# V of B by one load per head, with an 8 KB source element over four 2 KB destination rows

One core of one Trainium2 chip. The metric is the device time of one execution in microseconds (us), best read as the median of several; "the kernel before" and "the change" are run in turn on the same chip. The sets of experiments ran on different chips, so across sets only the ratios to "before" are compared. A run more than 1.5% above the fastest of its kernel is called slow and is left out of the ratios.

## The reference, cut to what matters

Two attention blocks read a key/value cache; their outputs are concatenated. Block A has 4 K/V heads shared by 32 query heads; block B has 32 heads, each with its own K and V, and it is B that moves the bytes.

```python
# B: x (16, 32, 1024), k_cache and v_cache (16, 32, 1024, 128), all bf16
q = (x @ wq).reshape(B, Sq, H, Dh).transpose(0, 2, 1, 3)
scores = jnp.einsum("bhqd,bhkd->bhqk", q, k_cache) * (Dh ** -0.5)
p = softmax(scores)
o = jnp.einsum("bhqk,bhkd->bhqd", p, v_cache)
return o.transpose(0, 2, 1, 3).reshape(B, Sq, H * Dh) @ wo
# ... A the same, with k and v repeated over 8 query heads; result = concatenate([A, B], -1)
```

K of B and V of B are 134 MB each; all else that is read comes to 69 MB.

## The kernel before: the parts that matter

The kernel does 128 steps. Each step handles one batch entry and four heads of B (and a piece of A). A step's K is one load of 1 MB; its V is two loads of 512 KB, two heads each. All loads are issued in order by one engine, SyncE (SP; its sequencer is "SPq" in the profile).

```python
# K of B: partition p gets 32 consecutive rows of one head: 8 KB in one piece on both sides
ksrc = pb["k"][q.b, q.h0:q.h0 + 4].rearrange("a (p s) d -> (a p) (s d)", s=32)
pr.add("sp", lambda e: e.dma_start(KB_sb[:, sl, :, :]..., ksrc), writes=[("KB", sl)], ...)

# V of B: partition p gets rows 8p..8p+7 of each head: 2 KB pieces on both sides
for t_ in range(2):
    vsrc = pb["v"][q.b, q.h0 + 2 * t_:q.h0 + 2 * t_ + 2].rearrange("a (p c) d -> p a c d", c=NCH)
    pr.add("sp", lambda e, ...: e.dma_start(VB_sb[:, sl, 2 * t_:2 * t_ + 2, :, :], vsrc),
           writes=[("VB", sl, t_)], dma_key=f"vb{sl}_{t_}", name="vb_dma", dur=2 * Sk * Dh * 2, ...)
```

K has two buffers (`NKB_SLOTS = 2`), V three. DVE transposes each K buffer into `KBt_sb`, and only then is it free for the next load; PE's product with V frees a V buffer. The program is not emitted in the order in which it is written: `list_schedule` gives every engine, and the issuer too, a fixed order at build time, by modelled durations (`dur`) and a modelled DMA rate.

```python
pr = pr.list_schedule()      # one fixed order for each engine, the issuer included
pr.finalize()                # semaphore waits that this order needs
```

## Time and profile before

| | before |
|---|---|
| time, median of the first 3 runs | 852.56 us (851.71 to 855.63) |
| span of the profiled run | 850.7 us |
| PE / DVE / ACT busy | 84% / 64% / 53% |
| DMA busy | 9 tenths or more in 39 of 40 slices, mean 401 GB/s |

The profile page of the kernel before: busy times; DMA busy in tenths and GB/s over 40 equal slices; packets by size; the one big queue; shares of the chain that ended last; and the two large loads with count, size and median time from issue to landing.

```profile
PE 713.5 (84%) x11974; PEld 435.7 (51%) x12104; DVE 546.6 (64%) x1117; ACT 447.0 (53%) x981; POOL 68.0 (8%) x76
...
DMA  9999999999999999999999999999999999999995
GB/s 350 377 411 398 410 412 408 410 412 400 413 405 401 414 412 415 408 401 413 403 414 413 409 411 411 414 389 412 411 409 415 411 411 413 411 391 414 403 407 219
DMA packets 127126, 341.52 MB, mean 401 GB/s; under 512 B 10016, under 2 KB 10528, under 8 KB 110624
...
q1 hardware_dynamic: 127008, 339.78, 101.2%
...
DMA 52%; PE 24%; DVE 17%; SPq 4%; issue 2%; ACT 1%; POOL 0%; DVEq 0%; POOLq 0%
...
KB_sb<-in_B_k_cache_dram SPq DMA_DIRECT2D x128, 1024.0 KB, 8.9
VB_sb<-in_B_v_cache_dram SPq DMA_DIRECT2D x256, 512.0 KB, 10.0
```

The DMA engines are busy from end to end, so the first reading is "bound by DMA". Two lines warn against stopping there. The queue's packets fill 101.2% of 16 engines' span: consecutive packets overlap a little in the records. The chain that ended last is half DMA. The waits of the issuer (microseconds in total, times, longest):

```profile
SPq L802 <- DVE KBt_sb L837: 142.8, 40, 9.1
SPq L802 <- DVE stat L900: 76.7, 26, 5.9
SPq L809 <- POOL VAp_sb L811: 70.7, 28, 5.7
```

Line 802 issues K of B: it stands and waits until DVE has emptied a K buffer. While the queue is long, such a wait costs nothing.

The view of V's tile gives one issue of V as 469 ns at the median (shortest, median and longest in ns):

```profile
L817 SPq DMA_DIRECT2D VB_sb<-in_B_v_cache_dram x256: 367/469/3536, 16.6 to 830.1; - x128
```

The trace also keeps every DMA packet. Of the kernel before it has 100,096 packets of 2 KB (65,536 of them V of B), median 84 ns, and 16,384 of 8 KB for K of B, median 309 ns, so 77 ns per 2 KB. The intent of the change is this difference.

### The profile page before, as it was taken

To read this page: it belongs to the slowest core of one execution; us is meant where nothing else is said; L and a number is where in the kernel's file an instruction comes from. 1 tells how busy PE (TensorE), PEld (TensorE's weight loads), DVE (VectorE), ACT (ScalarE), POOL (GpSimd) and SP (SyncE) were. 2 spreads that over 40 slices of the span, in tenths; PEclk is the share of its full clock that TensorE was granted. 3 is DMA by queue.
4 is the path that set the end of the run, shared out by engine and by line. 5 is a ranking of instruction groups with operands and counts; after the bars stand their busy time and mean duration, and the time that the engine had idled before them with its cause. 6 is when DMAs were issued, how large, how long until landed. Compare 5 with 4: busy or idle time off the path is not lost.

```text
span 850.7 us, 27284 instructions
## 1 busy us (share of the span) xinstructions
PE 713.5 (84%) x11974; PEld 435.7 (51%) x12104; DVE 546.6 (64%) x1117; ACT 447.0 (53%) x981; POOL 68.0 (8%) x76
## 2 busy tenths in 40 slices
PE   3999999799979797788997878887999768787876
PEld 2556655456546464455654445553555535454543
DVE  0655677467755677567774757675677756767774
ACT  1456666456645465445744445563566535645452
POOL 0000000000001000010000000000000000000000
PEclk9999999999999999999998999998999999999998
DMA  9999999999999999999999999999999999999995
GB/s 350 377 411 398 410 412 408 410 412 400 413 405 401 414 412 415 408 401 413 403 414 413 409 411 411 414 389 412 411 409 415 411 411 413 411 391 414 403 407 219
DMA packets 127126, 341.52 MB, mean 401 GB/s; under 512 B 10016, under 2 KB 10528, under 8 KB 110624
## 3 DMA queue, kind: packets, MB, share of 16 engines
q1 hardware_dynamic: 127008, 339.78, 101.2%
q8 instruction: 95, 1.56, 0.6%
q14 instruction: 23, 0.19, 0.1%
HBM read 337.64 MB, written 2.10 MB: 399 GB/s over the span
## 4 chain that ended last, share of the span: by engine, by line
DMA 52%; PE 24%; DVE 17%; SPq 4%; issue 2%; ACT 1%; POOL 0%; DVEq 0%; POOLq 0%
DMA KB_sb<-in_B_k_cache_dram 33%; DVE KBt_sb L837 13%; PE ps_pj L667 8%; DMA VA_sb<-in_A_v_cache_dram 5%; PE ps_s L872 4%; DMA VB_sb<-in_B_v_cache_dram 3%; DMA wq_sb<-in_B_wq_dram 3%; PE ps_pj L724 3%; PE ps_kt L930 3%; DMA wq_sb<-in_A_wq_dram 2%; PE ps_o L964 2%; PE ps_pt L914 2%; SPq L817 2%; PE ps_s L855 1%; DMA woB_sb<-in_B_wo_dram 1%
## 5 line engine op out<-in xcount | busy, mean ns | idle before, releaser
L837 DVE STREAM_TRANSPOSE KBt_sb<-KB_sb 128x1024 f32<-128x1024 f32 x256 | 306.5, 1226 | 78.0 <-DMA KB_sb<-in_B_k_cache_dram 73.1
L895 ACT ACTIVATE P_sb<-ps_s 128x512 bf16<-128x512 f32 x256 | 152.1, 599 | 94.7 <-PE ps_s L872 80.1
L887 ACT ACTIVATE PTA_sb<-ps_s 128x1024 bf16<-128x1024 f32 x128 | 131.3, 1026 | 99.2 <-PE ps_s L855 79.0
L872 PE MATMUL ps_s<-KBt_sb,QB_sb 32*32 32x512 bf16 x4096 | 144.6, 388 | 13.8 <-ACT P_sb L895 7.9
L667 PE MATMUL ps_pj<-xT_sb,wq_sb 128*128 128x512 bf16 x404 | 115.3, 396 | 16.7 <-DMA wq_sb<-in_B_wq_dram 4.4
L597 ACT COPY PT_sb<-ps_pt 128x512 f32<-128x512 f32 x128 | 75.0, 586 | 103.3 <-PE ps_o L964 90.1
L811 POOL COPY VAp_sb<-VA_sb 128x1024 bf16<-128x1024 bf16 x64 | 66.6, 1040 | 764.2 <-DMA VA_sb<-in_A_v_cache_dram 739.9
L914 PE MATMUL ps_pt<-id,P_sb 128*128 128x128 f32 x512 | 101.4, 301 | 11.4 <-ACT P_sb L895 8.4
L964 PE MATMUL ps_o<-VB_sb,PT_sb 128*32 128x128 bf16 x4096 | 81.8, 222 | 23.6 <-DMA VB_sb<-in_B_v_cache_dram 18.9
L914 PEld LDWEIGHTS ps_pt<-id,P_sb 128*128 128x128 f32 x512 | 80.8, 206 | 31.1 <-ACT P_sb L895 13.8
L964 PEld LDWEIGHTS ps_o<-VB_sb,PT_sb 128*32 128x32 bf16 x4096 | 60.3, 97 | 59.1 <-issue 55.0
L855 PE MATMUL ps_s<-QT_sb,KTA_sb 128*128 128x256 bf16 x512 | 84.0, 273 | 7.5 <-ACT PTA_sb L887 4.0
L930 PE MATMUL ps_kt<-VAp_sb,PTA_sb 128*128 128x129 bf16 x1024 | 78.8, 224 | 7.6 <-POOL VAp_sb L811 4.7
L872 PEld LDWEIGHTS ps_s<-KBt_sb,QB_sb 32*32 32x32 bf16 x4096 | 48.9, 89 | 68.4 <-ACT P_sb L895 12.6
L980 DVE TENSOR_SCALAR OB_sb<-ps_o,rinv_all 128x128 bf16<-128x128 f32 x128 | 43.7, 341 | 61.7 <-PE ps_o L964 61.0
L930 PEld LDWEIGHTS ps_kt<-VAp_sb,PTA_sb 128*128 128x128 bf16 x1024 | 66.3, 100 | 31.8 <-POOL VAp_sb L811 12.8
L667 PEld LDWEIGHTS ps_pj<-xT_sb,wq_sb 128*128 128x128 bf16 x448 | 42.2, 110 | 47.7 <-issue 7.2
L724 PE MATMUL ps_pj<-woB_sb,OTB_sb 128*128 128x512 bf16 x193 | 58.3, 388 | 9.0 <-ACT OTB_sb L597 2.6
L855 PEld LDWEIGHTS ps_s<-QT_sb,KTA_sb 128*128 128x128 bf16 x512 | 44.8, 98 | 31.5 <-ACT PTA_sb L887 7.9
L900 DVE TENSOR_TENSOR stat<-stat 64x1 f32<-64x1 f32 x256 | 44.8, 175 | 23.7 <-ACT P_sb L895 15.7
L724 PE MATMUL ps_pj<-woA_sb,OTA_sb 128*128 128x512 bf16 x198 | 51.5, 379 | 6.9 <-DMA woA_sb<-in_A_wo_dram 2.3
L735 DVE TENSOR_TENSOR acc<-acc,ps_pj 128x512 f32<-128x512 f32 x64 | 43.0, 672 | 19.0 <-PE ps_pj L724 18.8
(52 smaller groups left out, 520.5 us busy)
## 6 DMA issues: line engine op xcount, KB each, us to landing
KB_sb<-in_B_k_cache_dram SPq DMA_DIRECT2D x128, 1024.0 KB, 8.9
VB_sb<-in_B_v_cache_dram SPq DMA_DIRECT2D x256, 512.0 KB, 10.0
KA_sb<-in_A_k_cache_dram SPq DMA_DIRECT2D x64, 256.0 KB, 9.9
VA_sb<-in_A_v_cache_dram SPq DMA_DIRECT2D x64, 256.0 KB, 8.4
wq_sb<-in_B_wq_dram SPq DMA_DIRECT2D x16, 512.0 KB, 10.0
woB_sb<-in_B_wo_dram SPq DMA_DIRECT2D x32, 256.0 KB, 10.7
woA_sb<-in_A_wo_dram SPq DMA_DIRECT2D x32, 256.0 KB, 8.9
wq_sb<-in_A_wq_dram SPq DMA_DIRECT2D x12, 512.0 KB, 10.6
```

The costliest lines, as they stand in the source:

```text
L597: pr.add("act", lambda e: e.copy(dst_ap, src_ap), reads=reads, writes=writes, name=name + "@act", wtag=wtag, rtag=rtag)
L667: last = e.matmul(ps_pj[:, 0:NTOK], pick(src, j), xT_sb[:, pi, j, :], start=(j == 0), stop=(j == DJ - 1))
L724: last = e.matmul(ps_a[:, 0:OUTW], OT[:, gp, hh, :], wo_[:, hh, oh * OUTW:(oh + 1) * OUTW], start=(hh == 0), stop=(hh == nh - 1))
L811: pr.add("pool", lambda g: g.tensor_copy(VAp_sb[:, sl, :, 0:Dh], VA_sb[:, :, :]), reads=["VA"], writes=[("VAp", sl)], name="VAp_cp", rtag= ...
L837: pr.add("dve", lambda e: e.transpose(KBt_sb[:, sl, t_, :].bitcast(F32).rearrange("p (s r i) -> p s r i", r=2, i=32), KB_sb[:, rs, t_, :]. ...
L855: last = e.matmul(ps_s[:, sbf, c2, i * 2 * P:(i + 1) * 2 * P], KTA_sb[:, sl, c * P:(c + 1) * P], qt, start=True, stop=True)
L872: last = e.matmul(ps_s[32 * cg:32 * cg + 32, sbf, g, :].rearrange("p (sh cl j) -> p sh cl j", sh=4, cl=4), lhsT, kt[32 * a:32 * a + 32, g, ...
L887: pr.add("act", lambda e: e.activation(dst, src, ACTF.Exp, scale=scale), writes=BK_S[sbf] + [("PTA", q.half)], name="expA", rtag={("Sv", s ...
L895: pr.add("act", lambda e, src=src, dst=dst, g=g: e.activation(dst, src, ACTF.Exp, scale=scale, accum_out=st[:, g:g + 1]), writes=[BK_S[sbf ...
L914: last = e.transpose(ps_pt32[:, m * P:(m + 1) * P], p32[:, m:Sk // 2:NPK], id32[:])
L930: last = e.matmul(ps_kt[:, qh * OA0:qh * OA0 + Dh + 1], PTA_sb[:, h, c, qh * P:(qh + 1) * P], VAp_sb[:, sl, 4 * h + c, 0:Dh + 1], start=(h ...
L964: last = e.matmul(ps_o[32 * a:32 * a + 32, 0:Dh], PT_pairs[:, c // 2, 32 * (a ^ (c // 4 * 2)):32 * (a ^ (c // 4 * 2)) + 32, c % 2], VB_sb[ ...
```

## The change

Each head of V is loaded by itself. The source is described as 32 rows of 8 KB (what four neighbouring partitions will hold), the destination as 128 rows of 2 KB; the copy instruction is built directly because the two shapes differ. Each pattern is written with two dimensions.

```diff
+def folded_load(e, dst, src):
+    inst = mybir.InstDMACopy(
+        name=..., mode="Copy", engine=mybir.EngineType.SP, queue="qSPDynamicHW",
+        ins=e.lower_ap_dma(src), outs=e.lower_ap_dma(dst))
+    return e.add_instruction(inst)
...
-for t_ in range(2):
-    vsrc = pb["v"][q.b, q.h0 + 2 * t_:q.h0 + 2 * t_ + 2].rearrange("a (p c) d -> p a c d", c=NCH)
-    pr.add("sp", lambda e, ...: e.dma_start(VB_sb[:, sl, 2 * t_:2 * t_ + 2, :, :], vsrc), writes=[("VB", sl, t_)],
-           dma_key=f"vb{sl}_{t_}", name="vb_dma", dur=2 * Sk * Dh * 2, ...)
+for t_ in range(4):
+    vsrc = pb["v"][q.b, q.h0 + t_].rearrange("(g p c) d -> g (p c d)", p=4, c=NCH)
+    pr.add("sp", lambda e, ...: folded_load(e, VB_sb[:, sl, t_, :, :].rearrange("p c d -> p (c d)"), vsrc), writes=[("VB", sl, t_)],
+           dma_key=f"vb{sl}_{t_}", name="vb_dma", dur=Sk * Dh * 2, ...)
...
-    pr.add("pe", ..., reads=["PT", ("VB", kvs, 0), ("VB", kvs, 1)], name="PVB", ...)
+    pr.add("pe", ..., reads=["PT"] + [("VB", kvs, a) for a in range(4)], name="PVB", ...)
```

So three things change at once: the form of the packets (I call it the fold), the number of loads (256 become 512), and, because the scheduler sees other operations, the fixed order of all engines.

More of the change, by code (lines that the diff above doesn't have):

```diff
@@ L491, in general_program @@
     return pr
+def folded_load(e, dst, src):
+    inst = mybir.InstDMACopy(
+        name=e.bass.get_next_instruction_name(), mode="Copy", engine=mybir.EngineType.SP, queue="qSPDynamicHW",
+        ins=e.lower_ap_dma(src), outs=e.lower_ap_dma(dst))
+    return e.add_instruction(inst)
 def build(nc, pa, pb, out):
@@ L814, in st_dmaV @@
                 sl = q.vslot
-                for t_ in range(2):
-                    vsrc = pb["v"][q.b, q.h0 + 2 * t_:q.h0 + 2 * t_ + 2].rearrange("a (p c) d -> p a c d", c=NCH)
-                    pr.add("sp", lambda e, t_=t_, vsrc=vsrc: e.dma_start(VB_sb[:, sl, 2 * t_:2 * t_ + 2, :, :], vsrc), writes=[("VB", sl, t_)],
-                           dma_key=f"vb{sl}_{t_}", name="vb_dma", dur=2 * Sk * Dh * 2, wtag={("VB", sl, t_): q.kid})
+                for t_ in range(4):
+                    vsrc = pb["v"][q.b, q.h0 + t_].rearrange("(g p c) d -> g (p c d)", p=4, c=NCH)
+                    pr.add("sp", lambda e, t_=t_, vsrc=vsrc: folded_load(e, VB_sb[:, sl, t_, :, :].rearrange("p c d -> p (c d)"), vsrc), writes=[("VB", sl, t_)],
+                           dma_key=f"vb{sl}_{t_}", name="vb_dma", dur=Sk * Dh * 2, wtag={("VB", sl, t_): q.kid})
         def st_ktrA(q):
@@ L967, in st_pv @@
             for c0 in range(0, NCH, 2):
-                pr.add("pe", lambda e, c0=c0: e_pv(e, c0), reads=["PT", ("VB", kvs, 0), ("VB", kvs, 1)], writes=[BK_O], name="PVB",
-                       dur=0.116, tag="B%d" % q.t, rtag={"PT": q.qid, ("VB", kvs, 0): q.kid, ("VB", kvs, 1): q.kid}, wtag={"Ops": q.qid})
+                pr.add("pe", lambda e, c0=c0: e_pv(e, c0), reads=["PT"] + [("VB", kvs, a) for a in range(4)], writes=[BK_O], name="PVB",
+                       dur=0.116, tag="B%d" % q.t, rtag=dict([("PT", q.qid)] + [(("VB", kvs, a), q.kid) for a in range(4)]), wtag={"Ops": q.qid})
         def st_recip(q):
```

## The prediction

> **What bounds it now.** The DMA engines. In the page's 40 slices DMA busy is 9 in all but the last, at about 400 to 414 GB/s; 341.5 MB move in the 850.7 us span. PE is busy 84%, DVE 64%, ACT 53%. Landing takes 8.9 to 10 us, several times a transfer's own 1.3 to 2.5 us, so work is always queued; only 16 of 423 windows of 2 us have fewer than 15.5 packets in flight on average, which loses about 8 us, nearly all at the two ends. The chain that ended last names PE (24%) and DVE (17%) beside DMA (52%): loads wait for buffers, but the queue does not run dry.
>
> **Packet records of the same trace.** V of B is 65,536 packets of 2,048 B, median 84 ns; K of B is 16,384 packets of 8,192 B, median 309 ns, that is 77 ns per 2 KB. The difference fits about 9 ns per packet plus 27.3 bytes per ns. A semaphore packet (16 per DMA) takes 9 ns. Packets overlap (the sum is 101.2% of 16 engines' span), so not all of it is pitch: filling the saturated span with a sum of packets gives an estimated pitch of 80.8 ns for 2 KB and 311 to 314 ns for 8 KB.
>
> **What the change does.**
> - If an 8 KB source element with four 2 KB destination elements behaves as one 8 KB packet: 16,384 x (4 x 80.8 - 314 to 311 ns) / 16 engines = 9.5 to 12.5 us less. By records (4 x 84 - 309 = 27 ns) it would be 27 us, the far end.
> - Added: 256 more DMAs, 4,096 semaphore packets of 9 to 11 ns: 2.3 to 2.8 us on 16 engines.
> - Issue: two of 469 ns per step become four of perhaps 350 ns (K's take 340 ns): about +60 us on the issuer, which has room.
> - Bytes, PE, ACT and DVE work are unchanged. PV waits for the last of four semaphores instead of two: the same moment. The recomputed static schedule may shift a microsecond or two.
>
> The Trainium skill, "DMA: Bandwidth & Descriptors", section "Why small descriptors are slow", gives a fixed ~3-cycle overhead per packet inside the engine; this trace agrees in kind (2 KB packets cost 2 to 9 ns more per 2 KB than 8 KB ones). Its section "The descriptor swizzle" gives an engine partitions 0-3 and 32-35: groups of four neighbours, so a four-partition source element can stay on one engine and port. So I expect no port conflict; no trace here shows it yet.
>
> **On the path.** Nearly all DMA time is. Net 7 to 10 us of saving; later buffer waits take perhaps a fifth back. I expect 844 us, range 830 to 856. Faster by over 2% (below 835.5): 0.2; within 2%: 0.74; slower: 0.06.
>
> **What would show it.** Packets of 2 KB fall from 100,096 to about 34,560 and those of 8 KB double, at 309 to 315 ns; semaphore packets rise by 4,096; mean GB/s rises from 401 to about 405; DMA stays at 9; PE busy time is unchanged; V's issues become 512 of 256 KB at 0.33 to 0.4 us.
>
> **What would make it wrong.** The fixed cost sits on the destination element: then the 2 KB writes still pay, and the extra semaphores make it 1 to 3 us slower. Or the four writes of one read stall the engine or collide at a port (8 KB records well over 320 ns): slower by more. Or the record's 9 ns is all real pitch: 828 us. Or PE, at 84%, begins to bound and the queue runs dry in mid-span.

## The result, and the profile after

| | before | the change |
|---|---|---|
| median, first set | 853.77 us (4 runs) | 850.97 us (849.28 to 852.18, 4 runs) |
| ratio, first set | 1 | 0.9965 (95%: 0.9941 to 0.9989) |
| ratio, second set (6 runs of the change) | 1 | 1.0005 (0.9981 to 1.0029) |
| ratio, third set (6 runs) | 1 | 0.9950 (0.9927 to 0.9973) |

A ratio is the mean time of one kernel's fast runs over that of the other's fast runs of the same rounds, so it is not quite the ratio of the medians quoted. The three ratios average 0.9973, about 2 us of 853: the same by the 2% rule, and the gain is a quarter of the 7 to 10 us in the prediction. (The 844 us of the prediction is 8.6 below the 852.56 then known; its own sum, 7 to 10 less a fifth, would be 5.6 to 8.)

The same lines of the page for the change:

```profile
PE 722.7 (85%) x12104; PEld 430.9 (51%) x12104; DVE 544.4 (64%) x1117; ACT 448.5 (53%) x981; POOL 68.2 (8%) x76
...
DMA  9999999999999999999999999999999999999995
GB/s 346 384 389 404 410 397 398 414 403 391 411 414 417 417 409 415 414 382 403 419 414 415 412 417 418 409 411 417 419 420 415 407 417 419 408 390 410 418 413 195
DMA packets 82075, 341.59 MB, mean 402 GB/s; under 512 B 14112, under 2 KB 14624, under 8 KB 49184
...
q1 hardware_dynamic: 81952, 339.80, 99.3%
...
DMA 48%; PE 28%; DVE 12%; SPq 6%; issue 3%; ACT 2%; POOL 0%; POOLq 0%; DVEq 0%
...
KB_sb<-in_B_k_cache_dram SPq DMA_DIRECT2D x128, 1024.0 KB, 8.6
VB_sb<-in_B_v_cache_dram SPq DMA_DIRECT2D x512, 256.0 KB, 8.5
```

The packets did what was intended: those of 2 KB up to 8 KB fell from 100,096 to 34,560 (under 8 KB less under 2 KB), and the folded ones are recorded as one packet of 8 KB, median 309 ns, as K's are. The packets now fill 99.3% of the engines' span instead of 101.2%. But the mean rate is 402 GB/s and not 405. The best slices are faster (420 against 415), and the deepest dip in mid-run is deeper (382 against 389). PE's busy time in the two pages is not comparable to the microsecond: 130 matmul records are missing from the trace of before (11,974 against 12,104).

One dip, read closely, in the change. The issuer's timeline (start, duration, instruction) and DMA share with GB/s in four stretches around it; after the start and end of a stretch come its length, the busy times of PE, PEld, DVE, ACT and POOL, the granted clock, the DMA share and GB/s.

```profile
369.79 0.33 SPq L809 DMA_DIRECT2D KB_sb<-in_B_k_cache_dram  x1
371.02 0.33 SPq L816 DMA_DIRECT2D VA_sb<-in_A_v_cache_dram  x1
371.40 3.03 SPq L498 DMA_DIRECT2D VB_sb<-in_B_v_cache_dram  x5
378.51 0.33 SPq L809 DMA_DIRECT2D KB_sb<-in_B_k_cache_dram  x1
```

```profile
374.00:377.50 3.50, 3.16 (x25) 2.40 (x22) 2.55 (x7) 0.95 (x2) 0.00 (x0) 0.80 1.00 403
377.50:379.50 2.00, 1.58 (x36) 0.71 (x36) 2.00 (x4) 1.58 (x3) 1.04 (x1) 1.00 0.63 235
379.50:382.00 2.50, 2.50 (x27) 1.70 (x20) 2.50 (x3) 1.31 (x5) 0.00 (x0) 1.00 0.95 328
382.00:388.00 6.00, 5.79 (x104) 3.63 (x102) 3.97 (x11) 3.37 (x8) 0.00 (x0) 1.00 1.01 406
```

The waits of the issuer between 366 and 396 us name what held the K load back:

```profile
SPq L809 <- DVE KBt_sb L844: 12.9, 3, 6.5
```

From 374.4 to 378.5 us the issuer issues nothing, because no K buffer is free. By 377.5 only 0.6 MB of issued bytes are left, by 378.5 only 0.25 MB with 8 packets in flight instead of 16, and the DMA engines fall to 0.63 of their time. The packets that start just then are slow as well: ten that began between 379.5 and 380.0 took 900 to 1,096 ns instead of 309. This is the shape of the loss. The question is how much of it there is, and whether it is the cause.

Over the whole run of the change, the three largest waits of the issuer are shorter than before, not longer:

```profile
SPq L809 <- DVE KBt_sb L844: 101.2, 36, 7.7
SPq L809 <- DVE stat L907: 57.0, 30, 5.3
SPq L816 <- POOL VAp_sb L818: 42.8, 20, 6.1
```

All its waits come to 347 us, against 499 us before, while issuing V takes it 320 us instead of 160. So the loss cannot be read off the sum of these waits.

An account of the DMA engines answers how much. It is worked out from the packet records: back to back, a 2 KB packet of 84 ns starts 80 ns before the next, an 8 KB packet of 309 ns 306 ns before it. With these overlaps taken off, the number of packets in flight is 16.00 through most of the trace, so the account closes: span = pitch (each packet at its median less its overlap) + stalls (time of packets above their median) + idle (engines without a packet), all divided by 16, within 2 us. Here and below, each row is one profiled execution.

| profiled run | pitch, us | stalls, us | idle, us | stalls + idle | span, us |
|---|---|---|---|---|---|
| before | 824.5 | 12.0 | 12.8 | 24.8 | 850.7 |
| the change, first run | 811.8 | 20.4 | 15.9 | 36.3 | 849.6 |

The pitch fell by 12.7 us: 14.3 for the fold, less 1.2 for 4,096 more semaphore packets and 0.4 for sundry others. Stalls and idle time rose by 11.5.

### The profile page after: what moved, and what is told of

It reads as the page before. It is cut to its first block, busy times and chain, and to the rows that moved or that the text cites. A ratio compares the mean times of both kernels' runs of the same rounds, so it can differ in the third digit from the quotient of the medians.

```text
span 849.6 us, 27817 instructions
## 1 busy us (share of the span) xinstructions
PE 722.7 (85%) x12104; PEld 430.9 (51%) x12104; DVE 544.4 (64%) x1117; ACT 448.5 (53%) x981; POOL 68.2 (8%) x76
## 3 DMA queue, kind: packets, MB, share of 16 engines
q1 hardware_dynamic: 81952, 339.80, 99.3%
## 4 chain that ended last, share of the span: by engine, by line
DMA 48%; PE 28%; DVE 12%; SPq 6%; issue 3%; ACT 2%; POOL 0%; POOLq 0%; DVEq 0%
DMA KB_sb<-in_B_k_cache_dram 28%; DVE KBt_sb L844 9%; DMA VB_sb<-in_B_v_cache_dram 8%; PE ps_pj L674 7%; DMA woB_sb<-in_B_wo_dram 6%; PE ps_s L879 5%; DMA VA_sb<-in_A_v_cache_dram 4%; SPq L498 4%; PE ps_pj L731 4%; PE ps_o L971 3%; PE ps_kt L937 2%; PE ps_pt L921 2%; PE ps_s L862 2%; DMA KA_sb<-in_A_k_cache_dram 1%; DMA acc<-in_B_x_dram 1%
## 5 line engine op out<-in xcount | busy, mean ns | idle before, releaser
L902 ACT ACTIVATE P_sb<-ps_s 128x512 bf16<-128x512 f32 x256 | 151.8, 598 | 84.7 <-PE ps_s L879 73.7
L674 PE MATMUL ps_pj<-xT_sb,wq_sb 128*128 128x512 bf16 x448 | 121.0, 385 | 14.1 <-DMA wq_sb<-in_B_wq_dram 4.6
L937 PE MATMUL ps_kt<-VAp_sb,PTA_sb 128*128 128x129 bf16 x1024 | 76.4, 221 | 7.9 <-ACT KTA_sb L604 2.6
L937 PEld LDWEIGHTS ps_kt<-VAp_sb,PTA_sb 128*128 128x128 bf16 x1024 | 64.4, 98 | 33.5 <-POOL VAp_sb L818 12.9
L731 PE MATMUL ps_pj<-woB_sb,OTB_sb 128*128 128x512 bf16 x240 | 68.2, 390 | 7.5 <-DMA woB_sb<-in_B_wo_dram 5.2
L674 PEld LDWEIGHTS ps_pj<-xT_sb,wq_sb 128*128 128x128 bf16 x448 | 40.3, 108 | 50.2 <-DMA wq_sb<-in_B_wq_dram 7.7
L731 PE MATMUL ps_pj<-woA_sb,OTA_sb 128*128 128x512 bf16 x224 | 57.1, 379 | 3.7 <-DMA woA_sb<-in_A_wo_dram 1.9
L907 DVE TENSOR_TENSOR stat<-stat 64x1 f32<-64x1 f32 x256 | 41.9, 164 | 18.2 <-ACT P_sb L902 10.2
```

The costliest lines, as they stand in the source:

```text
L674: last = e.matmul(ps_pj[:, 0:NTOK], pick(src, j), xT_sb[:, pi, j, :], start=(j == 0), stop=(j == DJ - 1))
L731: last = e.matmul(ps_a[:, 0:OUTW], OT[:, gp, hh, :], wo_[:, hh, oh * OUTW:(oh + 1) * OUTW], start=(hh == 0), stop=(hh == nh - 1))
L902: pr.add("act", lambda e, src=src, dst=dst, g=g: e.activation(dst, src, ACTF.Exp, scale=scale, accum_out=st[:, g:g + 1]), writes=[BK_S[sbf ...
L937: last = e.matmul(ps_kt[:, qh * OA0:qh * OA0 + Dh + 1], PTA_sb[:, h, c, qh * P:(qh + 1) * P], VAp_sb[:, sl, 4 * h + c, 0:Dh + 1], start=(h ...
```

## The experiments

Theories at the outset. Schedule: the recomputed order gives most of the gain back. Issue: more and dearer issues keep the queue short. Stall (later called write): packets of this form stall by themselves. Later, from what these showed, queue or buffer: faster loads only run sooner into buffers that are not yet free.

### Set 1: form and order apart

e1 is the change unedited. e2 has its four loads and its order, but 2 KB elements on both sides; the orders of PE, DVE, ACT and POOL were checked to be equal. e3 and e4 keep the two operations per step for the scheduler and let each emit two loads, so that all engines keep the order of before, with folded loads (e3) or plain ones (e4).

```diff
 # e2, against the change
-folded_load(e, VB_sb[:, sl, t_, :, :]..., pb["v"][...].rearrange("(g p c) d -> g (p c d)", p=4, c=NCH))
+e.dma_start(VB_sb[:, sl, t_, :, :], pb["v"][...].rearrange("(p c) d -> p c d", c=NCH))
 # e3 and e4, against the kernel before
-pr.add("sp", lambda e, ...: e.dma_start(VB_sb[:, sl, 2 * t_:2 * t_ + 2, :, :], vsrc), ...)
+pr.add("sp", lambda e, t_=t_: [one_head(e, 2 * t_ + i) for i in range(2)], ...)   # each adds 16 to the pair's semaphore
```

> The change itself, unedited, as the anchor of this set. All theories: ratio 0.9965 again (0.994 to 0.999), about 3 us under the kernel before; packet time above the medians again about 20 us on 16 engines (12 us in the kernel before), idle DMA time again about 3 us more than before.

> One head per DMA as in the change, all engines in the change's order, but 2 KB elements on both sides. Schedule theory (the fold is worth 12 us of DMA time and the recomputed order gives 9 of them back): 862 to 865 us, about 10 us over the kernel before. Stall theory (the folded packets themselves stall more, the order is harmless): 855 to 857 us, 2 to 3 us over before from 4,096 more semaphore packets. Issue theory (the dearer issue of folded loads, 594 ns, drains the queue): 855 to 858 us, since plain 256 KB issues take about 430 ns.

> Folded loads, one head per DMA, but two of them per scheduled operation and one semaphore per pair, so that every engine runs in the order of the kernel before. Schedule theory: 842 to 845 us (10 us under before). Stall theory: 850 to 852 us, as the change; packet time above the medians stays near 20 us. Issue theory: 850 to 853 us, with DMA idle time at least 3 us over before, in stretches after waits of the issuer.

> One head per DMA with 2 KB elements on both sides, in the order of the kernel before: the splitting alone. All theories 855 to 857 us by 4,096 more semaphore packets (1.3 us of engine pitch, at most 2.3); more than 858 us would say that splitting itself (256 KB instead of 512 KB) costs, beyond its semaphores.

| | median, us | ratio to before (95%) |
|---|---|---|
| before | 853.01 | 1 |
| e1, folded, order of the change | 853.57 | 1.0005 (0.9981 to 1.0029) |
| e2, plain, order of the change | 856.99 | 1.0034 (1.0014 to 1.0054) |
| e3, folded, order of before | 847.40 | 0.9925 (0.9902 to 0.9948) |
| e4, plain, order of before | 854.53 | 1.0016 (0.9993 to 1.0040) |

In the order of before the fold is worth 0.9925/1.0016 = 0.991, 7.8 us of 853. Splitting alone costs 0.16%, 1.4 us, an interval that includes nothing. The order costs 0.18% with plain loads (1.0034/1.0016) and 0.8% with folded ones (1.0005/0.9925). The schedule theory as I had put it, 9 us whatever the loads, falls with e2, which was to be 862 to 865 us. But no theory had e3 right: it came out between the 842 to 845 us of the schedule theory and the 850 to 853 us of the others. e1 missed its ratio (0.994 to 0.999), and e4 came out just under its 855 to 857 us. The issue theory is weakened by e4: splitting took the issuer's time for V from 160 to 275 us and cost next to nothing.

The folded load is dearer to issue than I had thought. V's tile in e4, then in e3 (ns, shortest/median/longest):

```profile
L817 SPq DMA_DIRECT2D VB_sb<-in_B_v_cache_dram x512: 327/433/3163, 15.9 to 833.2; - x171
```

```profile
L499 SPq DMA_DIRECT2D VB_sb<-in_B_v_cache_dram x512: 471/594/2165, 16.4 to 829.9; - x171
```

594 ns for 256 KB, against 433 ns for the same bytes with equal elements. The account of e3 and e4, and of e1. The profiled run of e1 was the fastest of its six, that of e3 the slowest of its six (849.70 us, median 847.40):

| profiled run | pitch | stalls | idle | stalls + idle | span |
|---|---|---|---|---|---|
| e4, plain, order of before | 825.7 | 11.6 | 14.3 | 25.9 | 853.1 |
| e3, folded, order of before | 811.7 | 17.7 | 17.0 | 34.7 | 847.9 |
| e1, folded, order of the change | 811.8 | 19.6 | 12.8 | 32.4 | 845.6 |

From e4 to e3 the fold takes 14.0 us of pitch and gives 8.8 back as stalls and idle time, with the order of every engine unchanged. Since e3's profiled run was its slowest, 8.8 is the high end: by the ratios 14.0 became 7.8, so 6.2 came back. A recount by time shows that most idle time lies in the last 30 us of any run (9.9 us in e4, 9.6 in e3). Between the first and the last 30 us, idle time is 4.4 us in e4 and 7.3 in e3, stalls 10.5 and 15.8: what comes back is mostly long packets.

### Set 2: the loads alone

These four kernels load K and V of B in 128 steps and compute nothing; the results are wrong. They differ only in V's form.

```diff
-# the whole kernel
+for t in range(128):                      # three buffers each; an earlier landing in the same buffer is waited for
+    e.dma_start(KB_sb[:, sl, :], K as before).then_inc(ks[sl], 16)
+    for x in v_loads(e, sl, b, 4 * m):    # e5 pairs of heads 2 KB | e6 one head 2 KB | e7 folded | e8 as K, 8 KB on both sides
+        x.then_inc(vs[sl], 16)
```

> Wrong result on purpose: nothing but K of B (1 MB loads, 8 KB elements) and V of B in 128 steps, three buffers each, no compute; V as in the kernel before (two heads, 2 KB elements). From the pitches of the traces (80 ns per 2 KB packet, 306 ns per 8 KB packet, 5 ns per semaphore): 643 us of DMA time, with stalls and ends 650 to 656 us. Packet time above the medians about 6 ns per 8 KB packet, 0.6 ns per 2 KB packet, as in the whole kernel.

> Wrong result on purpose: the same with V one head per load, 2 KB elements. Semaphores alone add 1.3 us: 651 to 658 us, all theories.

> Wrong result on purpose: the same with V as in the change (8 KB source, four 2 KB destination elements). Pitch alone: 630 us. Stall theory (folded packets stall by themselves, 10 ns each or more): 16 us above the medians, 645 to 650 us, so only 5 us under the one-head plain loads. Issue or compute theory (the stalls and idle time come from a queue that the kernel lets run low): stalls under 8 us, 636 to 641 us, 14 us under.

> Wrong result on purpose: the same with V loaded as K is (1 MB, 8 KB elements on both sides). Pitch alone: 628 us. If every 8 KB packet stalls alike (about 6 to 8 ns each, whichever side is cut): 636 to 645 us and as many us above the medians as the folded form; if it is the four 2 KB writes that stall, the folded form has clearly more above the medians than this one.

| loads alone | median, us | mean GB/s in the page |
|---|---|---|
| e5, pairs, 2 KB | 678.80 | 400 |
| e6, one head, 2 KB | 680.11 | 399 |
| e7, one head, folded | 680.50 | 399 |
| e8, 8 KB on both sides | 649.65 | 417 |

All four missed their numbers upwards (by 5 to 30 us), and e7 missed in kind: with nothing but loads, the fold is worth nothing, while 8 KB on both sides is worth 30 us. Of the 8 KB packets of e7, about 40% took 336 to 344 ns; in the whole kernel 82% of them take 309 to 311 ns. Had I only these runs, I would have called the fold useless. They say that the 2 KB writes can set the rate; they do not say that they do so in the kernel, where e3 gains.

### Set 3: which engine's order

These use the change's own four operations and take some engines' orders from a schedule that sees two operations per step, the others from the change's. The order was verified for every engine.

```diff
-pr = pr.list_schedule()
+pr = in_order(pr, old)    # e10: all engines; e11: ("sp",); e12: ("pe", "act", "dve", "pool")
```

> The change itself once more, as anchor: its runs so far lie between 847 and 856 us, mean 852.0 us. Order theory: again 851 to 854 us. If it comes near 848 us, the difference of 5 us to the folded loads in the order of before was chance.

> The change with four separate loads and four semaphores per step as it has, but all engines in the order that the schedule gives with two loads per step. Order theory: 846 to 849 us, as the folded loads of the earlier run. Theory that one semaphore per pair made the difference: 851 to 854 us.

> The change with only the order of the loads on the issuer as with two loads per step; PE, DVE, ACT in the change's order. If the issuer's order (single V loads slipped between K loads and waits) costs the 5 us: 846 to 849 us. If the order of the computing engines costs them: 851 to 854 us.

> The reverse: PE, DVE and ACT in the order of two loads per step, the issuer in the change's order. If the issuer's order costs the 5 us: 851 to 854 us; if the computing engines' order costs them: 846 to 849 us.

| | median, us | ratio to before (95%) |
|---|---|---|
| e9, the change | 849.67 | 0.9950 (0.9927 to 0.9973) |
| e10, all engines in the order of before | 848.55 | 0.9935 (0.9903 to 0.9968) |
| e11, the issuer alone in the order of before | 872.43 | 1.0216 (1.0182 to 1.0250) |
| e12, the others alone in the order of before | 889.02 (887.57 without the slow run) | 1.0365 (1.0323 to 1.0408) |

e9 came out between its two forecasts, e10 as the order theory had it. They stand 0.15% apart here, against 0.8% in set 1, and the intervals overlap. Over both sets the folded loads average 0.9930 in the order of before (e3, e10), and over all three sets the change averages 0.9973: the order costs about 0.4%, 4 us, with an uncertainty nearly as large. Which engine's order it is cannot be told this way: e11 and e12 were each expected to run like one of the two parents, and mixing costs 18 and 31 us by the ratios. Here an order of loads and an order of their users were good only together. In e12 the stalls grew to 38 us and the idle time to 38 us by the account, nothing about the form of the packets being different. So stalls can come from the order alone.

The packet records show the same inside one run. Bytes queued are those issued less those of finished packets. In e3, an 8 KB packet stalls by 11.8 ns on average when 1.5 to 2 MB are queued, 6.7 ns at 2 to 2.5 MB, 3.6 ns at 2.5 to 3 MB and 2.2 ns at 3 to 4 MB. The median queue is 2.58 MB in the kernel before and 2.30 MB in e3. So stalls go with a short queue; that is a correlation. Of the 8 KB packets that stalled 300 ns or more in e3, 40% began within 12 ns of a moment when fewer than 16 packets were in flight; of the ordinary ones, 4%. The records do not name a packet's engine. But the dip above shows that some engines run out while others still have work: 8 packets in flight with 0.25 MB queued.

### Set 4: more room, and the forms one by one

e13 and e14 get a third K buffer; the 8 KB for it come from letting both blocks share one transposed x, which makes the kernel wrong by construction (the comparison passes it all the same, so it is no proof of that part). e13 has plain loads, e14 folded ones, in one order. e15 loads V alone in five forms, one after another. e16 is a right kernel that folds the other 2 KB loads with contiguous rows too.

```diff
 # e13, and e14 with e3's loads
-NKB_SLOTS = 2
+NKB_SLOTS = 3
-xT_sb = sb("xT_sb", [P, 2, DJ, NTOK], BF)
+xT_sb = sb("xT_sb", [P, 1, DJ, NTOK], BF)       # and index 0 for both blocks
 # e16, against e3; VA_sb, woA_sb and woB_sb likewise
-e.dma_start(KA_sb[:, sl, :, :], pa["k"][q.b, q.s].rearrange("(p c) d -> p c d", c=NCH))
+folded_load(e, KA_sb[:, sl, :, :].rearrange("p c d -> p (c d)"), pa["k"][q.b, q.s].rearrange("(g p c) d -> g (p c d)", p=4, c=NCH))
 # e15, against e7
-for t in range(128): K and V
+for form in ("wide", "both4k", "fold4", "fold2", "single"):
+    for _ in range(64): V in this form
```

> Wrong result on purpose (both halves share the transposed x of one, which frees 8 KB): the kernel before with three K buffers instead of two, V loads plain, two heads each. Queue theory: stalls fall from 12 us to under 6 us, 844 to 850 us. Write theory says nothing of this one.

> Wrong result on purpose, the same with V folded (one head per load, one semaphore per two heads, the same order on PE, DVE and ACT as with plain loads). Queue theory: with room in the queue the fold gives its pitch, 10 to 13 us under the plain form with three K buffers. Write theory: 0 to 6 us under it, and folded packets of 336 ns instead of 309 ns appear.

> Wrong result on purpose: V of B alone, no compute, 64 steps of 1 MB in each of five forms one after another, four buffers: 8 KB both sides, 4 KB both sides, 8 KB source with 2 KB destination, 4 KB source with 2 KB destination, 2 KB both sides. By pitch without stalls 157, 159, 157, 159 and 164 us each. Write theory: the two mixed forms take as long as 2 KB both sides (packets of about 336 and 168 ns), so 164 us each; queue theory: as long as the forms with the same source element.

> A right kernel that may beat both: V of B folded in the order of two loads per step, and K and V of A and both output weights folded too (24,576 more packets of 2 KB become 6,144 of 8 KB, no more loads, no more semaphores). By pitch 5.4 us less than the fold of V alone, which was 848 us: 843 us if pitch were all; queue theory: most of it is stalled away, 845 to 848 us; write theory: the same as the fold of V alone.

In e15, DMA share and GB/s in the steady part of each form, in the order 8 KB both sides, 4 KB both sides, 8 KB onto 2 KB, 4 KB onto 2 KB, 2 KB both sides (the last two numbers of a line):

```profile
20.00:150.00 130.00, 0.00 (x0) 1.00 1.01 422
180.00:315.00 135.00, 0.00 (x0) 1.00 1.03 410
345.00:490.00 145.00, 0.00 (x0) 1.00 1.02 387
530.00:670.00 140.00, 0.00 (x0) 1.00 1.03 387
710.00:840.00 130.00, 0.00 (x0) 1.00 1.05 387
```

In a lone stream the rate follows the smaller, destination element: 387 GB/s for all three forms that write 2 KB, whatever they read. The DMA share of 1.01 and more says that no form waited for its issues. All three are slower than a 2 KB packet of the whole kernel (84.7 ns of pitch here, from 16 x 2,048 B / 387 GB/s, against 80 ns there).

| | median, us | ratio to before (95%) |
|---|---|---|
| e13, plain, three K buffers | 855.94 | 1.0034 (1.0015 to 1.0053) |
| e14, folded, three K buffers | 847.85 | 0.9930 (0.9913 to 0.9947) |
| e16, all folded, order of before | 848.46 | 0.9946 (0.9927 to 0.9966) |

With three K buffers the fold, splitting included, is worth 0.9930/1.0034 = 0.990, 8.9 us; without, e3 is 6.4 us under before, with intervals of about 2 us on either. This 8.9 lies between the forecasts of the two theories (10 to 13 us, and 0 to 6), and almost none of e14's 8 KB packets (0.06%) took 336 to 344 ns. It leans to the queue theory and does not prove it; its other half, that e13 would be 844 to 850 us, failed: the plain kernel did not get faster, and its stalls stayed at 12.2 us. Nor did the folded one: e14 stands at 0.9930, e3 and e10 at 0.9925 and 0.9935 with two K buffers, although the median queue grew to 3.1 MB in e13 and 3.0 MB in e14. The larger worth of the fold comes from a slower e13. This speaks against late K buffers as the only cause. e16 is no better than e3 and e10: another 5.3 us of pitch saved in the account (806.4 us) did not reach the clock.

### Set 5: less compute

If late buffers are the cause, then with the computing engines made light the fold must show its whole pitch; if the writes are the cause, it must show nothing, as in the lone stream. In both kernels the transposes of K are cut to a sixteenth and the projections halved. Their outputs are wrong, which doesn't matter for the times. Loads, waits and buffers stay. PE, DVE, ACT and POOL have one order in both; only V's loads differ, folded and split in e18 as in e3.

```diff
-e.transpose(KBt_sb[:, sl, t_, :]..., KB_sb[:, rs, t_, :]...)
+e.transpose(KBt_sb[:, sl, t_, 0:128]..., KB_sb[:, rs, t_, 0:128]...)
-for j in range(j0, j0 + JS):                    # input projection; the output projection likewise
+for j in ((j0 + 1,) if j0 + 2 == DJ else (j0,)):
```

> Wrong result on purpose: the kernel before with the DVE transposes of K cut to a sixteenth and the matmuls of the input and output projections halved; all waits, orders of the loads and their forms as before. If late buffers cost the stalls and the idle time: 840 to 846 us. If loads alone set the time and stalls are the memory's own: 851 to 854 us, as before.

> Wrong result on purpose: the same with V folded, one head per load. Buffer theory: with buffers free early the fold gives its 13 us (14.3 of pitch less 1.3 of semaphores), 827 to 833 us, at least 10 us under e17. Write theory: with the queue full the 2 KB writes set the rate as in the lone stream, 0 to 5 us under e17, and folded packets of 336 to 342 ns appear in numbers.

| | median, us | ratio to before (95%) |
|---|---|---|
| e17, light, plain | 849.69 | 0.9958 (0.9945 to 0.9972) |
| e18, light, folded | 839.89 | 0.9848 (0.9835 to 0.9861) |

Busy times and packets of e17, then of e18:

```profile
PE 639.1 (75%) x11473; PEld 396.1 (47%) x11592; DVE 301.2 (36%) x1117; ACT 446.4 (53%) x981; POOL 75.1 (9%) x80
...
DMA packets 127123, 341.47 MB, mean 403 GB/s; under 512 B 10016, under 2 KB 10528, under 8 KB 110624
```

```profile
PE 638.7 (76%) x11473; PEld 396.2 (47%) x11592; DVE 303.9 (36%) x1117; ACT 445.7 (53%) x981; POOL 75.0 (9%) x80
...
DMA packets 82069, 341.50 MB, mean 408 GB/s; under 512 B 14112, under 2 KB 14624, under 8 KB 49184
```

| profiled run | pitch | stalls | idle | stalls + idle | span |
|---|---|---|---|---|---|
| e17, light, plain | 824.3 | 7.5 | 14.9 | 22.4 | 848.0 |
| e18, light, folded | 811.4 | 10.9 | 13.8 | 24.7 | 837.6 |

The fold, splitting included, is now worth 0.9848/0.9958 = 0.989, 9.4 us, against 6.4 and 5.5 us for the same loads at full compute (e3, e10). The account shows where that comes from: 12.9 us of pitch saved and only 2.3 given back, where the same comparison at full compute, before to e3, saves 12.8 and gives back 9.9 (in e3's slowest run). By the ratios, 3.5 us come back at light compute and 6.4 (e3) or 7.3 (e10) at full. Each has an interval of about 2 us, so by time alone the difference is likely, not certain. The median queue is 2.9 MB in both. The issues are as dear as in e3 (594 ns), so dear issues by themselves are not enough, and the issue theory falls as the only cause. The folded packets do not slow to 336 ns here either, so the write theory falls as the main cause in the kernel. It keeps a share: 18% of e18's 8 KB packets take 1 to 9 ns more than the median, 2.0 us in all; in e17 almost none do.

I had expected 827 to 833 us for e18, at least 10 us under e17, and 840 to 846 us for e17. The difference came to 9.8 us by the medians; both lie higher, because making compute light helps the plain loads by only 3.5 us.

Two rivals remain. Light compute also takes away some of the traffic of DVE and PE in SBUF, so contention there could make the stalls. For DVE the trace of e3 speaks against it: 8 KB packets whose middle falls into a transpose are stalled 6.3 ns on average, the others 7.7 ns; for PE it was not tested. And the dear issue may still do its part at full compute. One folded load of 256 KB in 594 ns refills the queue at about 441 GB/s (an estimate from these two figures), little above the 402 GB/s that leave it. In e3, 5.8 of the 7.3 us of idle time in mid-run fall while the issuer is issuing, which it does 59% of the time. No run gives the folded loads a cheaper issue at full compute, so what late buffers and slow refilling each cost is not shown.

## Why the prediction was wrong, point by point

- **The bytes and packets: right; the pitch: undersized.** The packets came out as foreseen (34,560 of 2 KB, 8 KB doubled, median 309 ns). The fold's pitch was put at 9.5 to 12.5 us and is 14.3 by the better account. At light compute, 9.4 us net of the splitting reach the clock. That this lies within the predicted 7 to 10 is partly luck: a larger saving and a cheaper splitting, less 3.5 us that come back.
- **Splitting: oversized, if anything.** Put at 2.3 to 2.8 us; 1.2 us by the account, and 1.4 us by time (e4), with an interval that includes both zero and the forecast.
- **The step that failed** is "On the path. Nearly all DMA time is. Net 7 to 10 us of saving; later buffer waits take perhaps a fifth back." The part of the sum that was mis-sized is the "fifth". At full compute in one fixed order, 6.2 of 14.0 us come back by the ratios and 8.8 in the account of one run (e4 to e3), so 44% to 63%; at light compute 3.5 and 2.3 of 12.9 (e17 to e18), so 18% to 27%. In the change as it stands, 11.5 of 12.7 us came back, the effect of the order included. The DMA digits of 9 showed that the engines were always occupied. They did not show packets that took longer than their median. A queue of 2.6 MB looked ample as an average; in e3 it is 2.3 MB, and the shorter it is, the more its packets stall. That lighter compute brings the saving back is what e17 and e18 show; that it does so through late buffers is argued.
- **"The recomputed static schedule may shift a microsecond or two": undersized.** 1.5 us with plain loads (e2 against e4), about 4 us with folded ones on average, 1 to 7 in single sets. Together with the item before, this leads from the 7 to 10 us forecast to about 2.
- **Issue of 0.33 to 0.4 us: wrong.** It is 0.594 us. It does not take the saving away by itself (e18); a part at full compute is not ruled out.
- **Mean rate of 405 GB/s: wrong**, 402, for the same reason as the time. DMA at 9 throughout: right, and no evidence.
- **No port conflict: consistent with the runs.** The result is right, and 82% of e3's 8 KB packets, K's and the folded ones, take 309 to 311 ns. Of the alternatives, "the fixed cost sits on the destination element" fits the lone stream (e15). In the kernel it is worth at most about 2 us, if the 1 to 9 ns of set 5 come from it, which no run shows.

**What the Trainium skill said, and what the runs say.** "DMA: Bandwidth & Descriptors", section "Why small descriptors are slow (HBM only)", gives each packet a fixed overhead of about 3 cycles; the pitch here (80 ns per 2 KB, 306 ns per 8 KB) agrees in kind, 3.5 ns per 2 KB. The same page's section "The descriptor swizzle" lets an engine write partitions 0-3 and 32-35; no run here shows which engine wrote which partition. "Perfetto Trace Analysis", section "DMA Optimizations", says that batching small transfers into larger ones, 2 KB into 4 KB or 8 KB for example, "can dramatically improve throughput" and calls this the primary optimization when a kernel is DMA-bound. It speaks of transfers; what was enlarged here is the packet, within loads that became smaller. That gave 9% in a lone stream with 8 KB on both sides (422 against 387 GB/s), nothing in a lone stream with 8 KB on the source side only, and 0.3% in this kernel.

**What stays open.** Why a folded packet runs at 306 ns of pitch in the kernel and at 4 x 84.7 ns in a stream of nothing else: the runs show both, and none tells the cause. In the loads-only kernels all 16 engines keep closer together (V's first and last engine land 0.7 us apart in e7, 2.45 us in the change), which may matter; that was not tested. What the remaining stalls of 7.5 to 12 us in the plain kernels are. And which engine's order costs the 4 us, and whether late buffers or slow refilling of the queue takes the saving back at full compute.

The folded loads in the order of before (e3, e10) are a right kernel and the best found: 0.9925 and 0.9935, 5 to 6 us under before and some 4 under the change. It beats both, by less than 1%.

## What to carry to other kernels

A DMA row full of nines says that the engines hold packets, not that a cheaper packet will shorten the run: look at the queue's depth, at packets longer than their median, and at whether the issuer waits for buffers, and expect part of a saving on the loads to come back as long packets and idle time while compute keeps its pace: here 6 to 9 us of 14. When a change alters the operations that a static scheduler sees, run its loads in the old order too; moving only some engines to the other order cost 18 and 31 us here. Test a form of load both alone and in place: here the lone stream said "nothing", and the kernel in its old order said "5 to 8 us".

## What the Trainium skill lacked or had wrong

- "DMA: Bandwidth & Descriptors", section "Why small descriptors are slow (HBM only)": it does not say which side's element counts when the two differ. In a lone stream 8 KB or 4 KB read onto 2 KB writes in SBUF ran at 387 GB/s, exactly as 2 KB on both sides, while 4 KB and 8 KB on both sides ran at 410 and 422 GB/s. So in a lone stream the small element on the SBUF side alone cost it. In the whole kernel it did not show: folded packets took 309 ns, as K's did.
- No page has the issue time of a load with unequal elements: 594 ns for 256 KB, against 433 ns with 2 KB on both sides and 340 ns for 1 MB with 8 KB on both sides.
- "Perfetto Trace Analysis", section "DMA Optimizations": it does not say that a saving on the packets can come back as stalls and idle time while the DMA row stays full. Here 14.0 us of packet time saved became 7.8 us at full compute in the same order.
